# Three hundred and eighty-four bytes in front of the first tile of an attention and mixer kernel

## The chip, the core and the metric

The kernel runs on one core of one Trainium2 chip. The core has a matrix engine (TensorE, PE in the profile; its weight loads are listed apart as PEld), a vector engine (VectorE, DVE), an activation engine (ScalarE, ACT), a general engine (GpSimd, POOL), and a queue engine (SyncE, SP) that issues DMA transfers. They work side by side and wait for each other by semaphores. All of them read and most of them write SBUF, the working memory: 128 partitions, each a row of bytes. A tile takes the same stretch of bytes in every partition, so one number, its first byte, says where it lies. TensorE writes to PSUM, another memory, which this change doesn't touch.

The metric is the device time of one execution in microseconds (us), the median of several runs.

## What is computed

The reference, cut to its core (B = 4 batches, H = 8 heads, S = 576 rows, D = 64; d_model 512, w_tok1 576x256, w_tok2 256x576, w_ch1 512x1536, w_ch2 1536x512; all float32):

```python
q_rot, k_rot = (rotate(q), rotate(k))
scores = scale * np.matmul(q_rot, k_rot.transpose(0, 1, 3, 2))
scores = scores - np.max(scores, axis=-1, keepdims=True)
attn = np.exp(scores)
attn = attn / (np.sum(attn, axis=-1, keepdims=True) + 1e-09)
attn_out = np.matmul(attn, v)
...
x = attn_out.transpose(0, 2, 1, 3).reshape(B, S, H * D)
xt = x.transpose(0, 2, 1)
h = np.maximum(xt @ w_tok1, 0.0) @ w_tok2
u = x + h.transpose(0, 2, 1)
h2 = np.maximum(u @ w_ch1, 0.0) @ w_ch2
return u + h2
```

## The kernel before

It has three stages. **Attention** takes the 32 heads as 16 pairs: q and k come in by DMA (lines 410, 414), are rotated, transposed by TensorE (L470) and copied to kt and qt; scores are float32 matmuls of 64 rows (L592); VectorE takes them out of PSUM into p while it keeps the row's extreme (L492), ScalarE makes the exponentials in place (L496), TensorE transposes them (L615), copies go to pt (L620), and pt times v follows (L633, five blocks of rows r = 0 to 4 by two heads). **The token mixer** (L818, L840) and **the channel mixer** (L935, L962) multiply in a form with a high and a low part: each float32 operand is split into two tiles of type float32r, and a product is three matmuls, high by high, high by low, low by high.

The channel mixer holds u transposed in tiles uh and ul for five chunks of rows (four of 512 and one of 256), walks over w_ch1 and w_ch2 in four groups g = 0 to 3, and keeps two sets of weights, c1h, c1l, c2h and c2l, that take turns: set 0 for g = 0 and 2, set 1 for g = 1 and 3. In each group and chunk the first product (L935: u streams, c1 is loaded as weights, 36 matmuls) goes through ScalarE and VectorE (L937, L939) into gh and gl, and the second (L962: c2 streams, g is loaded as weights, 9 matmuls for 128 rows) is added into X (L964). X is stored by DMA at the end (L970).

The order of work on every engine is written down: a planner (class Plan) runs at build time over a given list for the first two parts, and by its own costs for the rest. It knows tasks and buffers, and nothing of where a tile lies.

Tiles come from pools. Pools open either at the lower end of SBUF, and then each tile begins where the one before ended, or with side="right" at the upper end, growing down. The lower end holds const (ident, X, XT, stg and the scratch tiles fa, fh, fc), then first the attention pool (tabs, kraw, qraw, vraw, ..., kt, qt, p, pt, oT and small tiles) and, after that is closed, the channel mixer's wc (weight set 0, and uh and ul). The upper end holds a tile named edge of 88 floats, below it the token mixer's pool, and later the pool late in the same place (weight set 1, gh and gl). Every tile that a DMA writes or reads lies at the lower end.

The first bytes in the program as built, with the rest modulo 512:

```
tile                     first byte   modulo 512
ident                         16512          128
X0                            17024          128
stg0                          53888          128
kraw0                         74880          128
p0                           118400          128
pt0, pt1, pt2   141952, 153472, 164992   128, 384, 128
oT0                          176512          384
c1h0 (set 0)                  72320          128
c2h0 (set 0)                  84608          128
uh0                           96896          128
c1h1 (set 1, upper end)      179840          128
gh0 (upper end)              204416          128
```

All float32r tiles of both ends begin at 128 modulo 512, and each row or block of them that streams through TensorE begins at a multiple of 1024 bytes from the tile's first byte. In attention the streamed blocks fall on several rests: rows r of pt are 1280 bytes apart, so they alternate between 128 and 384, and the two halves of kt and of p are 1152 bytes apart.

Of the kernel before, what the change touches and what calls it, by code (L numbers as in the profile page):

```python
# [9 lines left out]
F32 = mybir.dt.float32  # L10
# [308 lines left out]
def rope_attention_mixer_kernel(ctx: ExitStack, tc: tile.TileContext, q, k, v, w_tok1, w_tok2, w_ch1, w_ch2, tab, out):  # L319
# [18 lines left out]
    P = 128  # L338
    plan = Plan()
    add = plan.add  # L340

    const = ctx.enter_context(tc.tile_pool(name="const", bufs=1))
    ident = const.tile([P, P], F32, name="ident")
    X = [const.tile([P, R, DM], F32, name=f"X{b}") for b in range(B)]
    XT = [const.tile([P, DM], F32, name=f"XT{c}") for c in range(B // 2)]
# [715 lines left out]
```

## Time and profile before

| | |
|---|---|
| median of 3 runs | 607.9 us (606.49, 607.9, 607.92) |
| profiled execution | 608.39 us |
| its span, first to last instruction | 606.6 us |
| mean granted TensorE clock | 0.996 |
| TensorE busy | 589.6 us (97%) |
| VectorE, ScalarE, GpSimd busy | 392.7, 309.3, 314.4 us |
| DMA | 36.15 MB, mean 60 GB/s |

How to read it: the span is what the profile sees; the profiled execution's own time is 1.8 us longer. An engine's busy share is an average over stages. Attention and the first token mixer fill about the first half of the span, the other token mixers and the channel mixer the rest.

### The profile page before, as it was taken

Reading aid. Unit: us, or ns where it says so; the run is one execution under the profiler, and the core shown is the slowest. Engines: PE = TensorE matmul, PEld = TensorE weight load, DVE = VectorE, ACT = ScalarE, POOL = GpSimd, SP = SyncE. Lnnn points to the kernel's source line nnn. Section 1 sums busy time; section 2 is a strip of 40 time slices with the busy share of each in tenths; the row PEclk is TensorE's granted clock in tenths of the full one; section 3 lists DMA queues with packets and bytes.
Section 4 is the critical chain, followed back from the end, with each engine's and each line's share of the span. In section 5 each row is a group of like instructions: output and inputs, shape, how many; then the busy total and the mean of one; then the engine's idle time right before and its main releaser. Section 6 shows DMA issues by size and latency. Waiting matters only on the chain.

```text
span 606.6 us, 12690 instructions
## 1 busy us (share of the span) xinstructions
PE 589.6 (97%) x4825; PEld 459.9 (76%) x4825; DVE 392.7 (65%) x1126; ACT 309.3 (51%) x787; POOL 314.4 (52%) x262
## 2 busy tenths in 40 slices
PE   4999999999999999989999999999999999999997
PEld 3677776867676767667787888888888888888886
DVE  5888989999999988689847546355423543223233
ACT  2799999999999998243445432233312321011110
POOL 4889689958977611133576786378602760000000
PEclk9899999999999999999999999999999999999999
DMA  5622333232322010011223221221101200001123
GB/s 152 192 61 58 99 84 85 61 84 78 86 81 64 8 54 6 24 26 27 70 61 79 71 61 53 59 72 52 53 1 35 71 1 1 0 1 69 70 69 105
DMA packets 34093, 36.15 MB, mean 60 GB/s; under 512 B 13808, under 2 KB 27632, under 8 KB 34032
## 3 DMA queue, kind: packets, MB, share of 16 engines
q1 hardware_dynamic: 33200, 35.01, 20.1%
q8 instruction: 38, 0.62, 0.4%
q10 hardware_dynamic: 832, 0.33, 0.2%
q14 instruction: 23, 0.19, 0.1%
HBM read 30.61 MB, written 4.72 MB: 58 GB/s over the span
## 4 chain that ended last, share of the span: by engine, by line
PE 88%; DVE 8%; issue 1%; ACT 1%; DMA 1%; DVEq 0%
PE m L935 24%; PE m L962 24%; PE s L633 11%; PE s L592 10%; PE s L615 6%; PE m L840 3%; DVE p L492 3%; PE m L818 2%; PE s L515 2%; PE s L470 2%; PE s L818 1%; PE s L662 1%; PE s L536 1%; PE s L840 1%; DVE X L667 1%
## 5 line engine op out<-in xcount | busy, mean ns | idle before, releaser
L937 ACT ACTIVATE gh<-m 128x512 fp32r<-128x512 f32 (+1 forms) x60 | 33.3, 555 | 168.9 <-PE m L935 168.3
L496 ACT ACTIVATE p<-p,nm 128x576 f32<-128x576 f32 x128 | 99.1, 781 | 6.5 <-DVE p L492 6.1
L939 DVE SCALAR_TENSOR_TENSOR gl<-m,gh 128x512 fp32r<-128x512 f32 (+1 forms) x60 | 38.2, 637 | 91.8 <-ACT gh L937 91.8
L964 DVE TENSOR_TENSOR X<-m,X 128x512 f32<-128x512 f32 (+1 forms) x65 | 44.4, 683 | 70.3 <-PE m L962 70.0
L935 PE MATMUL m<-uh,c1h 128*128 128x512 f32 (+1 forms) x240 | 88.6, 369 | 0.1
L935 PE MATMUL m<-ul,c1h 128*128 128x512 f32 (+1 forms) x240 | 88.4, 368 | 0.1
L935 PE MATMUL m<-uh,c1l 128*128 128x512 f32 (+1 forms) x240 | 88.3, 368 | 0.0
L592 PE MATMUL s<-kt,qt 64*128 64x288 f32 x512 | 84.7, 434 | 0.6 <-DVE pt L620 0.6
L962 PE MATMUL m<-c2h,gh 128*128 128x512 f32 (+1 forms) x219 | 84.6, 386 | 0.0
L962 PE MATMUL m<-c2l,gh 128*128 128x512 f32 (+1 forms) x219 | 84.6, 386 | 0.0
L962 PE MATMUL m<-c2h,gl 128*128 128x512 f32 (+1 forms) x219 | 84.6, 386 | 0.0
L633 PE MATMUL s<-pt,vraw 128*64 128x256 f32 (+1 forms) x640 | 84.5, 411 | 0.0
L720 POOL TENSOR_TENSOR fa<-fc,fa 128x512 f32<-128x512 f32 (+3 forms) x32 | 37.7, 1178 | 62.3 <-DVE fa L718 60.0
L633 PEld LDWEIGHTS s<-pt,vraw 128*64 128x64 f32 x640 | 43.2, 137 | 31.6 <-DVE p L492 2.7
L620 ACT COPY pt<-s 128x256 f32<-128x256 f32 (+1 forms) x175 | 61.7, 407 | 10.6 <-PE s L615 9.5
L492 DVE TENSOR_SCALAR_CACHE_REDUCE p<-s,nm 128x288 f32<-128x288 f32 x128 | 63.0, 510 | 3.3 <-PE s L592 0.2
L615 PEld LDWEIGHTS s<-ident,p 64*128 64x128 f32 x1152 | 48.3, 139 | 20.1 <-ACT p L496 5.4
L712 POOL TENSOR_SCALAR fa<-fa 128x512 f32<-128x512 f32 (+2 forms) x30 | 51.6, 1724 | 16.3 <-ACT fa L708 16.2
L492 DVE TENSOR_SCALAR_CACHE_REDUCE p<-s 128x288 f32<-128x288 f32 x128 | 54.6, 451 | 7.3 <-PE s L592 6.6
L592 PEld LDWEIGHTS s<-kt,qt 64*128 64x128 f32 x512 | 49.8, 194 | 8.6 <-DVE pt L620 1.1
L615 PE MATMUL s<-ident,p 64*128 64x64 f32 x1152 | 54.4, 227 | 1.9 <-DVE p L492 0.5
L935 PEld LDWEIGHTS m<-uh,c1h 128*128 128x128 f32 x240 | 45.2, 188 | 8.0 <-DVE ul L915 0.3
(132 smaller groups left out, 1066.2 us busy)
## 6 DMA issues: line engine op xcount, KB each, us to landing
stg<-in_moe_w_ch_dram SPq DMA_DIRECT2D x16, 384.0 KB, 3.2
stg<-in_moe_w_ch_dram SPq DMA_DIRECT2D x12, 512.0 KB, 3.6
vraw<-in_v_dram SPq DMA_DIRECT2D x16, 256.0 KB, 3.7
kraw<-in_k_dram SPq DMA_DIRECT2D x15, 256.0 KB, 3.0
qraw<-in_q_dram SPq DMA_DIRECT2D x15, 256.0 KB, 3.2
out_dram<-X SPq DMA_DIRECT2D x15, 256.0 KB, 2.3
stg<-in_moe_w_tok_dram SPq DMA_DIRECT2D x4, 512.0 KB, 4.7
kraw<-in_k_dram SPq DMA_DIRECT2D x32, 32.0 KB, 2.6
```

The costliest lines, as they stand in the source:

```text
L492: return lambda: nc.vector.tensor_scalar(out=p()[:, c * W2:(c + 1) * W2], in0=sb.t[:, 0:W2], scalar1=-D ** -0.5, scalar2=nm.t[:, 0:1] if c ...
L496: return lambda: nc.scalar.activation(out=p(), in_=p(), func=ACTF.Exp, bias=nm.t[:, 1:2], scale=-1.0, accum_out=l())
L592: nc.tensor.matmul(sbs[h].t[:, 0:W2], flat(qt.t)[halves[h], TL + j * P:TL + (j + 1) * P], flat(kt.t)[halves[h], TL * (1 - h) + u * W2:TL * ...
L615: nc.tensor.transpose(xy[z].t[:, i * TL:(i + 1) * TL], pb.t[halves[z], c0:c0 + P], ident[halves[z], halves[z]])
L620: return lambda: e(out=pt[c].t[:, R * h:R * h + m, o + z * TL:o + (z + 1) * TL], in_=xy[z].t[:, 0:m * TL].rearrange("p (r s) -> p r s", r=m))
L633: nc.tensor.matmul(ab.t[halves[h], 0:w], vb.t[:, h, r, :], m, start=(r == 0), stop=(r == R))
L712: clamp = lambda e: lambda: e.tensor_scalar(out=A(), in0=A(), scalar1=EXP_LO, scalar2=EXP_HI, op0=ALU.max, op1=ALU.min)
L720: mul_ = lambda e: lambda: e.tensor_tensor(out=A(), in0=C(), in1=A(), op=ALU.mult)
L935: nc.tensor.matmul(tb.t[:, 0:n], a, m, start=(i == 0), stop=(i == len(lst) - 1))
L939: y = add("DVE", dve(n), lambda f=f, tb=tb: nc.vector.scalar_tensor_tensor(out=gb.t[1][:, f, 0:n], in0=tb.t[:, 0:n], scalar=0.0, in1=gb.t[ ...
L962: nc.tensor.matmul(tb.t[:, 0:w], a, m, start=(i == 0), stop=(i == len(lst) - 1))
L964: y = add("DVE", dve(w) + 0.08, lambda u=u, tb=tb, cols=cols, w=w: nc.vector.tensor_tensor(out=u[:, cols], in0=tb.t[:, 0:w], in1=u[:, cols ...
```

## The change

One line. A tile of 96 floats, 384 bytes in each partition, is taken from the pool const ahead of ident and used by nothing.

```diff
--- before
+++ after
@@ -340,6 +340,7 @@
     add = plan.add
 
     const = ctx.enter_context(tc.tile_pool(name="const", bufs=1))
+    const.tile([P, 96], F32, name="pad")
     ident = const.tile([P, P], F32, name="ident")
     X = [const.tile([P, R, DM], F32, name=f"X{b}") for b in range(B)]
     XT = [const.tile([P, DM], F32, name=f"XT{c}") for c in range(B // 2)]
```

In the program as built after it, every tile of the lower end lies 384 bytes further up: ident at 16896, X0 at 17408, c1h0 at 72704, uh0 at 97280, all multiples of 512. Those that stood at 384 (pt1, oT and the first small tiles) come to 256, since tiles ahead of them have an odd number of half kilobytes. Tiles of the upper end stay where they were, at 128. The highest lower tile ends some 6 KB below the lowest upper one, so nothing overlaps. The sequences of instructions, operands and waits on the five engines are the same as before, instruction by instruction; only addresses differ.

## Rows read from the trace of the kernel before

**Rows 1.** The page's part 1: busy us by engine, share of the span, instructions.
```profile
PE 589.6 (97%) x4825; PEld 459.9 (76%) x4825; DVE 392.7 (65%) x1126; ACT 309.3 (51%) x787; POOL 314.4 (52%) x262
```

**Rows 2.** Stretches: us, busy us of PE, PEld, DVE, ACT, POOL; clock, DMA, GB/s.
```profile
0.00:15.00 15.00, 6.80 (x42) 4.90 (x44) 7.83 (x23) 4.19 (x13) 6.90 (x21) 1.00 0.58 151
15.00:295.00 280.00, 275.78 (x3284) 198.61 (x3282) 248.71 (x873) 225.47 (x625) 181.19 (x145) 0.99 0.24 66
295.00:606.60 311.60, 307.02 (x1509) 256.37 (x1505) 136.19 (x230) 79.66 (x151) 126.32 (x98) 1.00 0.16 49
```

**Rows 3.** The page's part 4, the chain that ended last, by engine.
```profile
PE 88%; DVE 8%; issue 1%; ACT 1%; DMA 1%; DVEq 0%
```

**Rows 4.** The chain in order of time, 422 to 497: start us, us, what.
```profile
422.75 8.16 PE m L935 x36
430.91 8.16 PE m L962 x36
439.07 4.31 PE m L935 x36
...
480.13 8.16 PE m L935 x36
488.29 8.16 PE m L962 x36
```

**Rows 5.** Groups by shape: line engine op, names, shapes, count | busy us, mean ns | idle.
```profile
L935 PE MATMUL m<-uh,c1h 128*128 128x512 f32 x192 | 74.8, 390 | 0.1
...
L935 PE MATMUL m<-uh,c1h 128*128 128x256 f32 x48 | 13.8, 287 | 0.0
```

**Rows 6.** TensorE in order of time, the second token product: start us, us.
```profile
283.92 0.61 PE L840 MATMUL m<-rs,w2h 128*128 128x512 f32 x2
...
284.60 0.61 PE L840 MATMUL m<-rs,w2h 128*128 128x512 f32 x2
...
285.28 0.61 PE L840 MATMUL m<-rs,w2h 128*128 128x512 f32 x2
```

**Rows 7.** TensorE in order of time: pt times v, two of the 32.
```profile
49.50 2.38 PE L633 MATMUL s<-pt,vraw 128*64 128x256 f32 x20
...
56.43 2.38 PE L633 MATMUL s<-pt,vraw 128*64 128x256 f32 x20
```

**Rows 8.** VectorE in order of time: scores taken out of PSUM into p.
```profile
29.86 0.46 DVE L492 TENSOR_SCALAR_CACHE_REDUCE p<-s 128x288 f32<-128x288 f32 x1 [0.31 <-PE s L592]
...
30.24 0.45 DVE L492 TENSOR_SCALAR_CACHE_REDUCE p<-s 128x288 f32<-128x288 f32 x1
...
33.71 0.52 DVE L492 TENSOR_SCALAR_CACHE_REDUCE p<-s,nm 128x288 f32<-128x288 f32 x1
...
34.15 0.51 DVE L492 TENSOR_SCALAR_CACHE_REDUCE p<-s,nm 128x288 f32<-128x288 f32 x1
```

**Rows 9.** The chain in order of time, 0 to 14: its DMA pieces and the first scores.
```profile
0.73 3.03 DMA tabs<-in_tab_dram
...
3.78 2.73 DMA kraw<-in_k_dram
...
10.32 3.94 PE s L592 x11
```

**Rows 10.** DMA: a queue's packets, MB, share; issues: KB each, us to landing.
```profile
q1 hardware_dynamic: 33200, 35.01, 20.1%
...
kraw<-in_k_dram SPq DMA_DIRECT2D x15, 256.0 KB, 3.0
...
kraw<-in_k_dram SPq DMA_DIRECT2D x32, 32.0 KB, 2.6
...
tabs<-in_tab_dram ACTq DMA_DIRECT2D x2, 128.0 KB, 3.2
kraw<-in_k_dram SPq DMA_DIRECT2D x2, 128.0 KB, 3.0
...
out_dram<-X SPq DMA_DIRECT2D x2, 128.0 KB, 2.1
```

## The prediction

> **What bounds the kernel now.** I read the page's busy line first: TensorE works 589.6 of 606.6 us, the next engine 392.7 [rows 1]. A mean can hide a stage with another limit, so the stretches come next: TensorE is busy 275.78 of 280 us up to 295 and 307.02 of 311.6 us after that, and only the first 15 us are thin, with 6.80 us of TensorE and the DMA engines at 0.58 [rows 2]. The chain that ended last is TensorE for 88%, VectorE 8%, DMA 1% [rows 3]. So the kernel is a stream of matmuls, and two questions decide: does a matmul's pace hang on where its operands lie, and does the start get shorter.
>
> The pace has to be read from starts, not from the mean durations of 390 and 287 ns [rows 5], since matmuls overlap. The chain gives 36 matmuls of 512 columns in 8.16 us, 226.7 ns each, and 36 of 256 columns in 4.31 us, 119.7 ns each [rows 4]. The difference is 107.0 ns for 256 columns, which is the 2.4 GHz level (106.7 ns) that the granted clock of 1.00 says. What is left is fixed: 226.7 - 213.3 = 13.3 ns in each matmul, whatever its width, or 32 columns.
>
> **What the change does.** It adds no instruction, no wait, no transfer. It moves each tile of the lower end by 384 bytes. 384 is three times 128, so whatever repeats every 128 bytes or less sees no difference: what can matter is a rest modulo 256, 512 or more, and the distance between a tile of one end and a tile of the other. I take four kinds of access in turn.
>
> *Float32 matmuls of attention.* They already run at several rests. In pt times v, the tile pt0 (49.50) has three of its five row blocks at 128 and two at 384, and pt1 (56.43) the reverse: both take 2.38 us [rows 7]. A block is four records (two heads, two records each); if each took 13 ns more at one rest than at the other, one of the two times would be 0.05 us longer. Price: 0. That the rest 0 itself is not among these blocks is left open by this row; the next one has it.
>
> *VectorE, ScalarE, GpSimd.* The scores go into p at four rests. At 29.86 (128) and 30.24 (384) the first half takes 0.46 and 0.45 us; at 33.71 (0) and 34.15 (256) the second half, which has one operand more, takes 0.52 and 0.51 us [rows 8]. So a write at a multiple of 512 is no faster than one at 256, nor 128 than 384. ScalarE's and GpSimd's accesses I price by this row too: 0. If one of them did gain, it would be hidden in the channel mixer, where VectorE has 136.19 and ScalarE 79.66 us of work in 311.6; in attention ScalarE is busy 225.47 and VectorE 248.71 of 280 us, so a loss there would show in part [rows 2].
>
> *DMA.* Every loaded or stored piece begins 128 bytes past a multiple of 256 before, and at one after. Queue q1 moves 33200 packets in 20.1% of 16 engines' span: 0.201 x 606.6 x 16 / 33200 = 58.8 ns for a packet of 35.01 MB / 33200 = 1055 bytes [rows 10]. Lower bound of a saving: 0 (no row has a packet at another rest, and none gives a reason for a loss). Upper bound: a whole part of 256 bytes less in each packet, 256 / 1055 x 58.8 = 14.3 ns. What of it is on the path is only the start: the chain waits 3.03 us for tabs and 2.73 us for kraw [rows 9], which together are the page's 1% of DMA; no later load stands on the chain. Before the first of these waits ends, three transfers of 128 KB land (two of tabs, one of qraw, as line 410 splits the first ones; pieces of 512 bytes, 256 of them each, 16 to an engine): 48 x 14.3 ns = 0.69 us. The second has one such transfer: 16 x 14.3 = 0.23 us. The last store adds 128 KB in pieces of 1024 bytes behind the span, 8 to an engine: 0.11 us. Upper sum 1.0 us. Which end is nearer? Loads of kraw land in 3.0 us with 256 KB, in 3.0 with 128 KB, in 2.6 with 32 KB [rows 10]: eight times the bytes cost 0.4 us, so the bytes' own time is a small part of a landing. I take 0.1 us.
>
> The Trainium skill (DMA: Bandwidth & Descriptors, "How a descriptor splits into AXI transactions") says that a descriptor that doesn't start at 256 bytes begins its first transaction at the boundary below, and that the unused bytes still cost time. By it a piece of 512 bytes at 128 costs 640 bytes' time, so the saving would be half of my upper bound, an estimate of 0.5 us in all; no row here shows such a piece alone.
>
> *Float32r matmuls of the mixers.* Weights that lie at different rests run at the same pace: in L840 the weights w2h and w2l of f = 0 lie at 128, of f = 1 at 384 (their halves are 2304 bytes apart), against streamed rs at 128. The groups of three begin at 283.92, 284.60 and 285.28, 0.68 us each [rows 6]. And set 1 at the upper end (422.75, 430.91) goes as set 0 at the lower one (480.13, 488.29), 8.16 us for 36 all four times [rows 4], so neither the end nor the distance of 100 KB counts as such. But every *streamed* float32r block lies at 128 modulo 512 before. No row shows one at 0. Price taken: 0, as in the float32 rows; its bounds are the two rivals.
>
> **Sum.** 608.39 us (the profiled execution) - 0 - 0 - 0.1 - 0 = 608.3. That execution lies 0.5 us above the median of 607.9, so the forecast is 607.8 us: no change that can be told. The three runs lie 1.4 us apart; about 0.3%, 1.8 us, is what a measurement of this kernel tells from no change.
>
> **Rival 1, faster: the fixed 13.3 ns is the misplaced start.** For: 13.3 ns is 32 columns, 32 columns of float32r are 128 bytes, and 128 is just the rest of every streamed block. A reader that fetched 512 bytes at a time from a multiple of 512 and dropped what lies ahead would give 512 + 32 and 256 + 32 columns, as measured. Against: the float32 blocks at 128 and 384 don't differ [rows 7]. They take four passes over the columns, so a lost start could hide there, which is why the rival lives. Its price: streamed from the lower end are uh and ul, 3 x (192 + 48) = 720 matmuls of L935 [rows 5], and set 0 of c2, two groups of 18 x 9 = 324 of L962; 1044 x 13.3 ns = 13.9 us, time 594.0. Part of it (a smaller block, say) gives anything down to there. Upper-end tiles stay at 128, so the rest of L962 would not gain.
>
> The Trainium skill (TensorE: Matmul & The Clock Gate, "Wait — 56ns, not 53.3ns?") puts the fixed part of a warm matmul at about 2.5 ns, 215.7 ns for 512 columns. The trace differs: 226.7. If the place were the reason for what is above the page's figure, 1044 matmuls would gain some 11 ns each, an estimate of 11.4 us, 596.5.
>
> **Rival 2, slower: the two ends fall out of step.** Before, operands of both ends share the rest 128; after, lower ones are at 0 and upper ones at 128. Where a matmul streams from one end while its weights come from the other, two reads that never met in one slice of memory could. That concerns L935 with set 1 (half of 720) and L962 with set 0 (324), 684 matmuls. Lower bound 0, by the L840 rows: weights 256 bytes out of step with the stream cost nothing [rows 6]. Upper bound: another fixed part, 13.3 ns each: 9.1 us, 617.0. It decides from 1.8 us / 684 = 2.6 ns a matmul on. That the out-of-step case which exists costs nothing speaks against it.
>
> **A third:** that the pad is never placed. The built program has every lower tile 384 bytes up, so this has no share of its own; it would give 607.9.
>
> **How the numbers follow.** No change, with 0 to 1.0 us of DMA and the runs' spread: 0.76, by itself 606.3 to 609.2. Faster by streaming, whole (0.06) or in part (0.07): 0.13, 594 to 606. Slower by rival 2: 0.11, 609.7 to 617. The first case reaches past -0.3% for 0.02 (both the DMA bound and the spread on one side). Faster 0.15, same 0.74, slower 0.11. Range 605.0 to 610.0: all of the first case and the near ends of the other two, which leaves some 0.2 outside.
>
> **What would show it.** In the changed kernel's chain, 36 matmuls of L935 and of L962 take 8.16 us, with either set. Rival 1 is right if L935 falls toward 36 x 213.3 = 7.68 us and L962 of groups 0 and 2 with it, while L962 of groups 1 and 3 stays. Rival 2 is right if L935 of groups 1 and 3 and L962 of groups 0 and 2 rise and the others don't. The start is right if the first scores begin at most 1 us earlier. If the time moves by more than 0.3% with all of these pieces unchanged, then attention moved, and my pricing of its engines from four rests of p was too narrow.

## The result: slower by half a per cent, and the profile after

The changed kernel takes 610.93 us, the median of 6 runs (609.76 to 612.9), against 607.91 us (606.49 to 608.85): ratio 1.0054, 95% interval 1.003 to 1.0078. The forecast was 607.8 us with a range to 610.0. Its own rival 2 is what happened. Lines of the changed kernel count one higher: L936 is the L935 of before, L963 the L962.

The page's busy line and the stretches, as in [rows 1, 2]:

```profile
PE 591.3 (97%) x4825; PEld 459.0 (76%) x4825; DVE 392.7 (65%) x1126; ACT 309.0 (51%) x787; POOL 314.2 (52%) x262
```
```profile
15.00:295.00 280.00, 275.79 (x3299) 199.24 (x3299) 249.90 (x873) 227.04 (x630) 182.02 (x145) 1.00 0.24 67
295.00:608.00 313.00, 308.41 (x1481) 254.59 (x1479) 133.91 (x227) 77.37 (x146) 125.17 (x97) 1.00 0.16 48
```

VectorE, ScalarE and GpSimd work as long as before, to 0.3 us. TensorE works 1.7 us longer with the same 4825 matmul records; the loss behind it is larger, since the profiled execution of before carries a stretch at a lower clock (below). Where the time goes, the chain in order of time says (start us, us, what), beside [rows 4]:

```profile
421.97 8.39 PE m L936 x36
430.36 8.17 PE m L963 x36
438.54 4.32 PE m L936 x36
...
463.32 8.17 PE m L936 x36
471.49 8.37 PE m L963 x36
479.86 8.17 PE m L936 x36
488.02 8.37 PE m L963 x36
```

The first three pieces are of group 1 (weight set 1, upper end), the others of group 2 (set 0, lower end). L936 with set 1 went from 8.16 to 8.39 us, L963 with set 0 from 8.16 to 8.37: just the two pairs in which stream and weights come from different ends. L936 with set 0 and L963 with set 1, both operands from one end, take 8.17. The piece of 256 columns, crossing too, takes 4.32 against 4.31. (Crossing is used below for a piece whose stream and weights lie at different ends.)

From the first L935 start to the last L962 start the channel mixer lasted 300.32 us before (302.56 to 602.88) and lasts 304.16 after (300.10 to 604.26):

```profile
302.56 0.39 PE L935 MATMUL m<-uh,c1h 128*128 128x512 f32 x1
...
602.88 0.28 PE L962 MATMUL m<-c2h,gl 128*128 128x256 f32 x1
```
```profile
300.10 0.40 PE L936 MATMUL m<-uh,c1h 128*128 128x512 f32 x1
...
604.26 0.28 PE L963 MATMUL m<-c2h,gl 128*128 128x256 f32 x1
```

That is the loss: 3.84 us. Counted by pieces: 8 of L936 with set 1 by 0.23 and 9 of L963 with set 0 (324 / 36) by 0.21 give 3.73; the rest is seams, 8.17 for 8.16.

In attention and the token mixer nothing changed its pace: pt times v [rows 7], the second token product [rows 6] and the scores' way into p [rows 8] read

```profile
47.05 2.38 PE L634 MATMUL s<-pt,vraw 128*64 128x256 f32 x20
...
53.98 2.38 PE L634 MATMUL s<-pt,vraw 128*64 128x256 f32 x20
...
281.43 0.62 PE L841 MATMUL m<-rs,w2h 128*128 128x512 f32 x2
...
282.11 0.62 PE L841 MATMUL m<-rs,w2h 128*128 128x512 f32 x2
```
```profile
27.41 0.46 DVE L493 TENSOR_SCALAR_CACHE_REDUCE p<-s 128x288 f32<-128x288 f32 x1 [0.19 <-PE s L593]
27.80 0.45 DVE L493 TENSOR_SCALAR_CACHE_REDUCE p<-s 128x288 f32<-128x288 f32 x1
```

with the blocks of pt now at 0 and 256, and p at 0 (27.41) and 256 (27.80). The token mixer's tiles all lie at the upper end, so none of its addresses changed; attention's tiles all moved together, so no distance inside attention changed.

The two profiled executions differ by less, 608.39 and 609.76 us, since in the one before TensorE's granted clock was at the 1.2 GHz level for part of the start (0.63 on the mean between 22 and 26 us, after four us with TensorE busy 3.22), and in the one after it stayed at 2.4 (1.00, after 3.59). Both kernels have executions with such a fall of the clock (mean 0.996 to 0.997) and without it (0.999 to 1.0), so the six times after fall into 611.99 to 612.9 and 609.76 to 609.87 us, and 26 of the kernel before, taken with the experiments, into 607.57 to 609.04 and 605.77 to 607.37; like with like the change costs 3.7 us with the fall (medians 612.0 and 608.3) and 3.6 without it (609.8 and 606.2).

### The profile page after: what moved, and what is told of

It is laid out like the page before. It is cut to its first block, busy times and chain, and to the rows that moved or that the text cites. A ratio compares the mean times of both kernels' runs of the same rounds, so it can differ in the third digit from the quotient of the medians.

```text
span 608.0 us, 12690 instructions
## 1 busy us (share of the span) xinstructions
PE 591.3 (97%) x4825; PEld 459.0 (76%) x4825; DVE 392.7 (65%) x1126; ACT 309.0 (51%) x787; POOL 314.2 (52%) x262
## 3 DMA queue, kind: packets, MB, share of 16 engines
q1 hardware_dynamic: 33200, 35.01, 20.1%
## 4 chain that ended last, share of the span: by engine, by line
PE 88%; DVE 8%; issue 1%; ACT 1%; DMA 1%; SPq 0%; DVEq 0%
PE m L936 25%; PE m L963 25%; PE s L634 11%; PE s L593 10%; PE s L616 6%; PE m L841 3%; DVE p L493 3%; PE m L819 2%; PE s L516 2%; PE s L471 1%; PE s L819 1%; PE s L663 1%; PE s L841 1%; PE s L537 1%; DVE X L668 1%
## 5 line engine op out<-in xcount | busy, mean ns | idle before, releaser
L936 PE MATMUL m<-uh,c1h 128*128 128x512 f32 (+1 forms) x240 | 89.1, 371 | 0.1
L936 PE MATMUL m<-ul,c1h 128*128 128x512 f32 (+1 forms) x240 | 89.0, 371 | 0.1
L936 PE MATMUL m<-uh,c1l 128*128 128x512 f32 (+1 forms) x240 | 88.9, 370 | 0.0
L963 PE MATMUL m<-c2l,gh 128*128 128x512 f32 (+1 forms) x219 | 85.3, 389 | 0.0
L963 PE MATMUL m<-c2h,gl 128*128 128x512 f32 (+1 forms) x219 | 85.2, 389 | 0.0
L963 PE MATMUL m<-c2h,gh 128*128 128x512 f32 (+1 forms) x219 | 85.2, 389 | 0.0
L616 PEld LDWEIGHTS s<-ident,p 64*128 64x128 f32 x1152 | 47.9, 139 | 20.3 <-ACT p L497 5.0
L616 PE MATMUL s<-ident,p 64*128 64x64 f32 x1152 | 54.2, 226 | 2.0 <-DVE p L493 0.5
L936 PEld LDWEIGHTS m<-uh,c1h 128*128 128x128 f32 x240 | 45.2, 189 | 8.5 <-DVE ul L916 0.3
```

The source lines that it names most:

```text
L616: nc.tensor.transpose(xy[z].t[:, i * TL:(i + 1) * TL], pb.t[halves[z], c0:c0 + P], ident[halves[z], halves[z]])
L936: nc.tensor.matmul(tb.t[:, 0:n], a, m, start=(i == 0), stop=(i == len(lst) - 1))
L963: nc.tensor.matmul(tb.t[:, 0:w], a, m, start=(i == 0), stop=(i == len(lst) - 1))
```

## The experiments

All vary bytes of unused tiles alone; instructions and their order stay. Theory 1: a float32r matmul slows when its weights are out of step with the streamed block, that is, when their first bytes leave different rests. (Within a piece the weights in use and those being loaded for the next matmul leave the same rest; which of the two counts, these runs do not separate.) The rivals are the place itself (a block at 0 is slow), the two ends, and attention.

**Both ends moved.**

```diff
+    const.tile([P, 96], F32, name="pad")
-    ... .tile([P, 88], F32, name="edge")
+    ... .tile([P, 120], F32, name="edge")
```

> Pad of 96 floats at the lower end and the upper end's edge tile widened from 88 to 120 floats: all float32r tiles of both ends begin at 0 modulo 512, in step again. Theory 1 (out of step): a 512-column float32r matmul goes from 226.7 to about 232.5 ns when the weights loaded beside it lie 128 bytes off the streamed block modulo 512; in step nothing is lost, so all pieces of 36 matmuls take 8.16 us and the time is that of before, 607 to 608 us. Theory 2 (the place itself): blocks at 0 are slower to read than at 128, so L936 and L963 show 8.37 us a piece with either set, and the time is 610 us or more.

Measured 608.02 us against 608.06, ratio 1.0004 (0.9989 to 1.0019). Its chain:

```profile
422.28 8.16 PE m L936 x36
430.44 8.16 PE m L963 x36
...
479.66 8.16 PE m L936 x36
487.82 8.16 PE m L963 x36
```

Every streamed block and every weight lies at 0, and nothing is lost: the place itself does not count. Rival 1 of the prediction falls too, since blocks at 0 keep the fixed 13.3 ns.

**The upper end alone** (edge of 120 floats, no pad).

> No pad at the lower end; the edge tile widened to 120 floats, so the upper end lies at 0 and the lower one at 128, the mirror of the change. Theory 1: L935 with set 1 and L962 with set 0 (the two pairs that cross the ends, 684 matmuls) take about 8.37 us for 36, the others 8.16; time 610 to 612 us, as with the change. Theory 2 (the place itself): the slow ones are those with a block at 0 in the stream or the weights, that is L962 with set 1 (both at 0) as well. If the sign of the offset counts, the crossing pieces stay at 8.16 and the time is before's.

611.87 us, ratio 1.0062 (1.0041 to 1.0083):

```profile
423.82 8.39 PE m L935 x36
432.21 8.18 PE m L962 x36
...
481.71 8.17 PE m L935 x36
489.87 8.37 PE m L962 x36
```

The mirror of the change costs the same, on the same pairs (8.39 and 8.37 us). The sign of the 128 bytes doesn't count.

**The pad between two tiles of one end.**

```diff
         sets = Slots([channel_set(wc, 0)])
+        wc.tile([P, 96], F32, name="pad")
         uT = [(wc.tile(...
```

> The 384 bytes stand inside the channel mixer's lower pool, between weight set 0 and the tiles uh and ul; all else lies as before. uh and ul come to 0, both weight sets stay at 128. Theory 1: every L935 piece of 36 matmuls, with set 0 (same end) as with set 1, takes about 8.37 us, and every L962 piece 8.16; 720 L935 matmuls, of which 576 have 512 columns, lose 5.8 ns each, 3.3 us, time about 611 us. Rival (the two ends): only L935 with set 1 is slow, half of that. Attention and the DMA transfers are as before in both.

611.16 us, ratio 1.0057 (1.0037 to 1.0077):

```profile
422.07 8.39 PE m L936 x36
430.46 8.18 PE m L963 x36
...
480.21 8.39 PE m L936 x36
488.60 8.18 PE m L963 x36
```

L936 is slow with either set, also where uh and c1 lie in one pool, and L963 is free. So the ends don't matter, only the distance between stream and weights. That what ScalarE and VectorE write into gh and gl is not the partner follows from the change itself: L936 with set 0 streams from 0 while gh lies at 128, and takes 8.17.

**The pad in front of attention's pool alone** (a tile of 96 floats ahead of tabs).

> The 384 bytes stand in front of attention's pool alone: tabs, kraw, qraw, vraw, kt, qt, p and pt lie at 0, while ident, X, stg and all tiles of the mixers lie as before. Theory 1: all channel mixer pieces take 8.16 us, and the time is before's or up to 1 us less, 606.5 to 608 us, since the first transfers begin at multiples of 512. Rival (attention pays too): the time is 609 us or more with unchanged channel mixer pieces.

606.91 us, ratio 0.9986 (0.9973 to 0.9999); all pieces of 36 with 512 columns take 8.16, but for the 8.19 behind a piece of 256 columns, as before. Attention pays nothing, though here ident stays at 128 while p comes to 0, so its transposes (L616) now have their two operands 128 bytes out of step: no loss shows in these float32 matmuls. This median is the lowest of all, but no gain is shown: seven of these twelve executions had no fall of the clock, against eight of the 26 before, and like with like it is 607.7 against 608.3 us with the fall and 606.7 against 606.2 without it.

**Eight more pads.** One line each, one profiled execution each, read by the pieces, since a single time can't be told from the fall of the clock:

```diff
+    const.tile([P, n], F32, name="pad")     n = 32, 64, 16, 8, 120, 112, 104, 88
     ident = const.tile([P, P], F32, name="ident")
```

> Pad of 32 floats: lower end at 256, upper at 128, so weights lie 128 bytes below the streamed block's rest (384 modulo 512) where L935 uses set 1 and L962 set 0. Theory 1 with a period of 256: those crossing pieces take the same 8.37 us for 36 as with the change. With a period of 512 the cost can differ from that of the change. All other pieces 8.16.

> Pad of 64 floats: lower end at 384, upper at 128, 256 bytes out of step. In the second token product 256 bytes out of step cost nothing before, so theory 1 with a period of 256 gives 8.16 us for all pieces. If 512 is the period, crossing pieces cost as much as at 128 bytes or more, 8.37 us and up.

> Pad of 16 floats: lower end at 192, upper at 128, 64 bytes out of step (weights 448 against the stream). If the loss depends on being out of step at all, crossing pieces take about 8.37 us; if it needs 128 bytes, 8.16.

> Pad of 8 floats: lower end at 160, upper at 128, 32 bytes out of step. As with 64 bytes: 8.37 us for crossing pieces if any step costs, 8.16 if it needs 128 bytes; between the two if the loss grows with the distance. Theory 2 (a block at 0 is slow) gives 8.16 here, since nothing lies at 0.

> Pad of 120 floats: lower end at 96, upper at 128, weights 32 bytes above the stream's rest where operands cross the ends. Theory 1 as it stands after eight runs (free at 0 and 256 bytes, 232.5 ns at 128 either way, 229 at -64, 233.3 at -32): if the sign doesn't matter, 512-column crossing matmuls take 233 ns, 8.40 us for 36, and the channel mixer lasts about 304.4 us from its first to its last matmul against 300.3. If the sign matters, anything between 8.0 and 8.5.

> Pad of 112 floats: lower end at 64, weights 64 bytes above the stream. Without a sign: 229 ns as at -64, about 8.25 us for 36 crossing matmuls, channel mixer 302 us. Rival (there is a distance at which the two reads miss each other): under 226.7 ns, under 8.16 us for 36.

> Pad of 104 floats: lower end at 32, weights 96 bytes above the stream. By the neighbours at 128 (232.5) and -64 (229): 230 to 233 ns, 8.28 to 8.39 us for 36 crossing matmuls. Rival (reads that miss each other): under 8.16 us.

> Pad of 88 floats: lower end at 480, weights 160 bytes above the stream (96 below modulo 256). If the period is 256 and the sign doesn't matter, as at 96 bytes: 230 to 233 ns, 8.28 to 8.39 us for 36 crossing matmuls. Rival (reads that miss each other): under 8.16 us.

A crossing piece of L936 and one of L963 in each, by where the lower end lies:

At 256:

```profile
423.36 8.39 PE m L936 x36
...
472.88 8.37 PE m L963 x36
```

At 384:

```profile
422.22 8.16 PE m L936 x36
...
471.44 8.16 PE m L963 x36
```

At 192:

```profile
421.64 8.26 PE m L936 x36
...
471.04 8.24 PE m L963 x36
```

At 160, with the crossing piece of 256 columns between the two:

```profile
424.25 8.40 PE m L936 x36
...
440.85 4.20 PE m L936 x36
...
473.74 8.39 PE m L963 x36
```

At 96:

```profile
424.93 8.40 PE m L936 x36
...
474.47 8.39 PE m L963 x36
```

At 64:

```profile
425.16 8.40 PE m L936 x36
...
474.61 8.40 PE m L963 x36
```

At 32:

```profile
424.82 8.43 PE m L936 x36
...
474.45 8.43 PE m L963 x36
```

At 480:

```profile
422.40 8.41 PE m L936 x36
...
472.09 8.40 PE m L963 x36
```

Expected were 8.37 or 8.16 at 192, about 8.25 at 64, and 8.28 to 8.39 at 32 and at 480; none of these four came out. Pieces that don't cross take 8.16 to 8.21 in all eight, so the odd places by themselves cost at most 0.05 us for 36.

Set out by the distance from the stream to the weights, modulo 256 bytes (us for 36 of L936, ns for one; first to last start of the channel mixer; the one run's time, where 192 and 480 had no fall of the clock at the start):

```
distance   36 of L936   one   channel mixer   run us
  0           8.16     226.7     300.32       607.91  (before, median of 6)
  0 (256)     8.16     226.7     300.32       607.85  (lower end at 384)
 32           8.40     233.3     304.51       612.83
 64           8.40     233.3     306.06       612.97
 96           8.43     234.2     305.24       613.18
128           8.39     233.1     304.16       610.93  (the change, median of 6)
128           8.39     233.1     304.21       611.13  (lower end at 256)
160           8.41     233.6     305.08       610.74
192           8.26     229.4     301.97       608.14
224           8.40     233.3     304.44       612.14
```

256 bytes apart is in step, so the period is 256, not 512. Every other distance tried costs a 512-column matmul 2.7 to 7.5 ns; 64 bytes one way costs much less than the other way, so the sign counts there, against what I expected. No distance tried runs a 512-column matmul under 226.7 ns on the mean, so for these the rival that two reads could miss each other falls. The crossing pieces of 256 columns went the other way: 4.20 us for 36 at 224, 4.24 at 64 and 192, 4.26 at 32 and 4.28 at 96, under the 4.31 in step, and 4.32 at 128 and 160. (In the run at 64 the clock stood at the lower level for 3.4 us inside the mixer, so its 306.06 holds more than the distance.)

## Why the prediction was wrong

**What bounds the kernel** was right, and so was the way to read it: a matmul's pace decides, and pieces of 36 tell it to 0.3 ns.

**Attention and the other engines, price 0**: right, by the pieces after and by the pad in front of attention alone. One reading behind it was off: the two heads of a row block r read rows r and r + 5 of pt, so each of the first four blocks has one head at either rest. Of the ten blocks of pt0 six lie at 128 and four at 384, which is the same difference of four records, so the 0.05 us stands.

**The failed step** is the price of the float32r matmuls, "Price taken: 0, as in the float32 rows", with the weight against rival 2 that "the out-of-step case which exists costs nothing". That case was 256 bytes [rows 6]. I had said myself that only what repeats at 256 or more can matter, and 256 bytes is in step under a period of 256: the row could not speak about 128. With it gone, no float32r row bore on rival 2, and 0.11 was too little for it. What the runs showed in place of the 0 is 6.4 ns for each of 288 matmuls of L936 and 5.8 ns for each of 324 of L963, 3.7 us.

**Rival 2** was right in its place: its test, L935 of groups 1 and 3 and L962 of groups 0 and 2 rising and the others not, came out to the piece. Its size was only bounded, 0 to 13.3 ns on 684 matmuls, 9.1 us; the cost came on the 612 of 512 columns alone, at about half the bound. Its name was too narrow: the pad between two tiles of the lower end does the same.

**Rival 1** is wrong: in step at 0 or at 128, the fixed part is 13.3 ns.

**DMA.** I took 0.1 us of at most 1.0. The queue's share didn't move from the 20.1% of [rows 10]:

```profile
q1 hardware_dynamic: 33200, 35.01, 20.1%
```

It is 19.3 to 20.1% in the four kernels whose attention tiles lie at multiples of 256 (the change, both ends moved, attention alone, lower end at 256) and 19.4 to 20.1% in the ten others, so no packet is seen to be shorter where tiles begin at a multiple of 256. The estimate of 0.5 us that followed from the Trainium skill (DMA: Bandwidth & Descriptors, "How a descriptor splits into AXI transactions") rested on shorter pieces, which this share does not show; the section tells its rule of what a transaction reads, and all of the queue's transfers but the stores write into SBUF. The start did get a little shorter: the first TensorE matmul begins at 4.71 to 4.91 us in the four aligned kernels and at 4.96 to 5.24 in the ten others, means 4.83 and 5.07. The first loads land sooner there, the 128 KB pieces of tabs in 2.8 to 2.9 us against 3.1 to 3.4 (3.2 before, [rows 10]):

```profile
tabs<-in_tab_dram ACTq DMA_DIRECT2D x2, 128.0 KB, 2.9
```

So 0.24 us is what the start gained, more than my 0.1 and within my bound; why these landings are shorter stays open.

So the sum is + 3.84 in the channel mixer, - 0.24 at the start, 3.6 us, as measured like with like.

## What to carry to other kernels

Where one float32r tile streams through TensorE in blocks of 512 columns and another gives the weights, let their first bytes agree modulo 256; a pad that moves only one pool can break a step that held by itself. What counted here was a relation between two addresses, and not a property of one. And a row that costs nothing at one distance says nothing about another until its period is known.

## What the runs showed of the hardware

A 512-column float32r matmul took 226.7 ns with stream and weights a multiple of 256 bytes apart, and 229.4 to 234.2 ns at the seven other distances tried. A 256-column one took 119.7 ns in step, 120.0 at 128 and 160 and 116.7 to 118.9 at the other five, so it lost next to nothing and mostly gained. That two reads meet in the memory is a likely reading of the loss, since only the distance of these two operands counts, but no run shows the meeting itself, and the gain at 256 columns does not follow from it. Why the two widths differ, and why 192 costs less than half of the rest, stays open.

The Trainium skill (SBUF — State Buffer, "A bandwidth-pool intuition that's wrong (but worth ruling out)") gives TensorE a second independent read port for weights and speaks of no limit that they share; the 6 ns of these runs, which come and go with the distance of the two operands, do not fit that, though whether the ports are where they arise is not shown.
